# Linear attention into a bilinear FFN on one core: k loads ahead of q, later scores of two units, a half out product ahead of a deferred one

## The chip, the core and the metric

The kernel runs on one core of one Trainium2 chip. The engines are TensorE (PE, matmuls; PEld is its weight load), VectorE (DVE), ScalarE (ACT), GpSimd (POOL) and SyncE (SP, which here issues nearly all DMAs). The metric is device microseconds of one execution; several executions are timed and the median is given. One execution was profiled, and all durations below are from it. Its span is the time from its first to its last instruction.

## The reference

There are 4 batches, 8 heads, 768 positions and a head size of 64. Attention is linear with a decay `lam` of each head and a running state over blocks of positions; the result, 3072 rows of 512, goes through a bilinear FFN of width 1536.

```python
for b in range(nb):                       # blocks of 64 positions
    intra = einsum('bhic,bhjc->bhij', qb, kb) * Dmask        # lam ** (i - j), lower triangle
    intra = einsum('bhij,bhjd->bhid', intra, vb)
    inter = einsum('bhid,bhde->bhie', qb * lam_pow, kv_state)
    out[:, :, sl] = intra + inter
    kv_state = lam_block * kv_state + einsum('bhsd,bhse->bhde', kb * rev_pow, vb)
x = out.transpose(0, 2, 1, 3).reshape(3072, 512)
return (x @ w_a) * (x @ w_b) @ w_out
```

## The kernel before

**Units and groups.** The 3072 rows are cut into 24 units of 128 rows (six to a batch). `GROUPS = (4, 1, 2, 4, 4, 4, 4, 1)` joins them for the FFN: group 0 has units 0 to 3, group 1 unit 4, group 2 units 5 and 6, groups 3 to 6 four units each (7 to 10, 11 to 14, 15 to 18, 19 to 22), group 7 unit 23. While the FFN of one group runs on PE, the attention of later units is woven in, so that the xT of a group (its attention result, transposed, as the matmuls take it) is ready when its FFN begins.

**The attention of a unit.** `P` in the plan is `prep_k` and `prep_v`. `prep_k` scales k and then q with powers of lam (L401, on POOL from unit 6 on) into one bf16 tile `qk`. For units 7 to 23 (`DMA_T`) it then issues a transposing DMA on SP (L429) that gives `qkT`. `prep_v` casts v (L420) and calls `pump`, which issues further loads on SP from the list `pending`, as far ahead as `LOOKAHEAD` lets it. Units 4 to 6 are transposed by PE (`T`, L443) and copied by ACT (L445). `S` is the scores: eight matmuls (L457) into two PSUM banks, then two masking multiplies on DVE (L480; with `MASK_ACT` one bank goes through a copy by ACT, L471, first). `V` updates the state (L527) and copies it. `O2` takes two units: matmuls with the state and with the masked scores (L497), then two casts into xT on ACT (L520). `Q` does this for units 7 and 8 together with the scores of 9 and 10.

**The FFN of a plain group (0, 1, 2, 7).** For each of twelve column blocks f: four matmuls with w_a into one PSUM bank, a cast by ACT (L605), four matmuls with w_b, a multiply on DVE into `ab` (L623). `ps_bank` hands out seven PSUM banks in rotation, and a matmul waits until the bank's former reader is done. Then come the out products (L643), twelve matmuls of 128x512 for each unit.

**The FFN of groups 3 to 6** (`ffn_z`) works on four units as a 2x2 block product with seven products instead of eight. It takes sums of weights (`WS`, `weight_sum`, L269 to L275, eight of them), sums of xT (`X`, `x_sums`, L713 to L726), and, for groups 4 to 6, sums of out weights (`WO`) and of the product (`SM`, `ab_sum`, L843 to L849). For each of six columns n, PE runs product 1 into U, 4 into V, 0 into W, 5 into U, 6 into V, 3 into U (L748, four matmuls of 128x256 each); ACT copies U and V in between into tiles of a pool of seven (`snap`, L829), and DVE subtracts such a copy from the finished bank (L777, L787, L789). Product 2 into U, the last of a column, is deferred into the next column: `last_product` is kept in `fin`, runs after the next column's product 5 (after its product 1 in "joined" groups), and ends with ACT's cast (L754) and DVE's multiply (L756). The out products of groups 4 to 6 are also seven products, each in two halves (`H`, `out_half`, L870, six matmuls of 128x256), woven into the next group; a group in which they are woven is joined.

**What sets the order.** Each engine runs its instructions in the order of the program, and that order is written out by hand: `PLAN` says at which slot of a group's FFN which piece of attention, sum or store is issued. In a plain group the slots 0 to 11 follow the column blocks and the later ones the parts of the out products; in groups 3 to 6 a column has three slots, the last three follow from 18 on. `WS_ENG` and its like say which engine takes a sum.

**Kept rows.** The FFN results of units 0 to 4 are copied by ACT into tiles of the same pool `snap` (`o_kept`, L634) and are stored only when the plan says `W` (`store_kept`, L629, on SP). Until such a store has landed, its tile can't be used for another copy of U or V.

Of the kernel before, what the change touches and what calls it, by code (L numbers as in the profile page):

```python
# [22 lines left out]
def _bc(ap, dims):  # L23
# [9 lines left out]
DMA_T = range(7, 24)  # L33
# [73 lines left out]
XS_ENG = {(3, 0): 'dve', (3, 1): 'dve', (3, 2): 'dve', (4, 0): 'dve', (4, 1): 'dve', (4, 2): 'dve', (5, 0): 'dve', (5, 1): 'pool', (5, 2): 'pool', (6, 0): 'pool', (6, 1): 'pool', (6, 2): 'pool'}  # L107
WS_ENG = {0: 'dve', 1: 'dve', 2: 'dve', 3: 'dve', 4: 'dve', 5: 'dve', 6: 'dve', 7: 'pool'}
WO_ENG = {0: 'dve', 1: 'dve', 2: 'pool', 3: 'dve', 4: 'dve'}
# [4 lines left out]
def kernel(  # L114
# [183 lines left out]
    for u in range(n0 + 1, NU):  # L298
        pending += [("q", u), ("k", u), ("v", u)]
    used = {"u": 0}  # L300
# [340 lines left out]
    def out_mms(op, ab, t, fs, lo=0, hi=d_model):  # L641
        for f in fs:
            nc.tensor.matmul(op[:, lo:hi], lhsT=ab[:, f, t * 128:(t + 1) * 128],  # L643
                             rhs=wo_sb[:, f, lo:hi], start=(f == 0), stop=(f == FC - 1))

    def ffn(u0, n, xT, hook, first, last):
# [36 lines left out]
        for t in range(n):  # L683
            op = ps_bank("op", [128, d_model], F32, ffn=True)
            if last and t == n - 1:
                for lo, hi in ((0, 256), (256, 384), (384, 512)):
                    if lo:
                        op = ps_bank("op", [128, d_model], F32, ffn=True)
                    out_mms(op, ab, t, range(FC), lo, hi)
                    store(u0 + t, op, lo, hi, nc.scalar if hi == d_model else None)  # L690
                return
            out_mms(op, ab, t, range(FC // 2))
            hook(FC + 2 * t)
            out_mms(op, ab, t, range(FC // 2, FC))
            store(u0 + t, op, 0, d_model)
            hook(FC + 2 * t + 1)
# [35 lines left out]
    def ffn_z(g, u0, xT, hook, joined, own):  # L732
# [27 lines left out]
        for n in range(NP):  # L760
# [5 lines left out]
            if joined:  # L766
                if fin:
                    fin.pop()()
                hook(3 * n)
# [332 lines left out]
```

## Time and profile before

| what | value |
|---|---|
| median of 3 timed runs | 224.38 us (224.23 to 226.21) |
| the profiled execution's own time | 223.83 us |
| its span | 222.1 us |
| PE busy | 213.9 us (96%) |
| DVE, ACT, POOL busy | 165.3, 122.7, 99.8 us |
| granted clock of TensorE | 1.000 |
| HBM read, written | 28.32 MB, 6.29 MB |
| DMA engines' busy share, 60 to 120 us | 1.20 to 1.26 |
| loads of q, k, v: each, issue to landing | 256 KB, 4.6, 4.7, 4.9 us |

A share of the DMA engines over 1 means that packets overlap on an engine. In a timeline a line gives the start and the length of a group of like instructions in us, engine, source line, operation, the tile written and the tiles read, how many, and in brackets the idle time of the engine just before, when it is over 0.15 us, with what ended it. Ends of matmuls are modelled, so starts are compared with starts. A few matmul records can be missing, so that a group may show one less than it has.

### The profile page before, as it was taken

Reading aid. Unit: us, or ns where it says so; the run is one execution under the profiler, and the core shown is the slowest. Engines: PE = TensorE matmul, PEld = TensorE weight load, DVE = VectorE, ACT = ScalarE, POOL = GpSimd, SP = SyncE. Lnnn points to the kernel's source line nnn. Section 1 sums busy time; section 2 is a strip of 40 time slices with the busy share of each in tenths; the row PEclk is TensorE's granted clock in tenths of the full one; section 3 lists DMA queues with packets and bytes.
Section 4 is the critical chain, followed back from the end, with each engine's and each line's share of the span. In section 5 each row is a group of like instructions: output and inputs, shape, how many; then the busy total and the mean of one; then the engine's idle time right before and its main releaser. Section 6 shows DMA issues by size and latency. Waiting matters only on the chain.

```text
span 222.1 us, 5601 instructions
## 1 busy us (share of the span) xinstructions
PE 213.9 (96%) x2225; PEld 159.0 (72%) x2235; DVE 165.3 (74%) x272; ACT 122.7 (55%) x249; POOL 99.8 (45%) x95
## 2 busy tenths in 40 slices
PE   7899999999999999999999999899999999999994
PEld 2476444448678657787547888688888888888994
DVE  0994773968798668889888889968688865777540
ACT  3686446038454266775356988776535666543322
POOL 6061004246795175540559559786417722051100
PEclk9999999999999999999999999999999999999999
DMA  4999999999999999999999999652021100112042
GB/s 132 321 265 349 356 387 344 277 216 218 216 204 220 232 174 248 190 275 245 180 248 236 233 201 211 138 101 50 0 88 56 52 0 4 47 47 97 0 145 94
DMA packets 99081, 39.42 MB, mean 177 GB/s; under 512 B 85488, under 2 KB 95088, under 8 KB 99056
## 3 DMA queue, kind: packets, MB, share of 16 engines
q1 hardware_dynamic: 98768, 39.00, 79.8%
q8 instruction: 17, 0.28, 0.6%
q10 hardware_dynamic: 288, 0.07, 0.1%
q14 instruction: 8, 0.07, 0.1%
HBM read 28.32 MB, written 6.29 MB: 156 GB/s over the span
## 4 chain that ended last, share of the span: by engine, by line
PE 67%; DMA 16%; SPq 5%; DVE 5%; ACT 2%; issue 2%; POOL 1%; ACTq 0%; DVEq 0%; POOLq 0%
PE U L748 17%; PE op L870 12%; PE V L748 9%; DMA wst<-in_moe_w_b_dram 8%; PE b_ps L596 5%; PE op L810 5%; PE a_ps L596 5%; PE W L748 4%; PE op L643 3%; DMA kf<-in_k_dram 3%; DMA k<-in_k_dram 3%; PE o_ps L497 3%; PE kq L457 2%; DMA out_dram<-o_kept 2%; SPq L187 1%
## 5 line engine op out<-in xcount | busy, mean ns | idle before, releaser
L829 ACT COPY u<-U 128x512 f32<-128x512 f32 x48 | 28.3, 590 | 16.5 <-PE U L748 16.4
L401 POOL TENSOR_TENSOR qk<-kf,lp_k 128x512 bf16<-128x512 f32 x18 | 19.5, 1084 | 33.7 <-DMA kf<-in_k_dram 18.9
L623 DVE TENSOR_TENSOR ab<-a_sb,b_ps 128x128 bf16<-128x128 bf16 (+2 forms) x48 | 19.2, 417 | 13.6 <-ACT a_sb L605 10.2
L596 PE MATMUL a_ps<-xT,wa_sb 128*128 128x128 bf16 (+2 forms) x198 | 27.6, 267 | 0.5 <-DVE wa_sb L244 0.2
L480 DVE TENSOR_TENSOR m<-kq,lotri 128x512 bf16<-128x512 f32 x40 | 25.6, 682 | 3.1 <-PE kq L457 3.0
L596 PE MATMUL b_ps<-xT,wb_sb 128*128 128x128 bf16 (+2 forms) x192 | 27.5, 272 | 0.2
L756 DVE TENSOR_TENSOR ab<-oab 128x1024 bf16<-128x1024 bf16 x24 | 19.0, 791 | 11.3 <-ACT oab L754 11.1
L401 POOL TENSOR_TENSOR qk<-qf,lp_q 128x512 bf16<-128x512 f32 x20 | 24.8, 1242 | 1.7 <-DMA qf<-in_q_dram 1.7
L605 ACT CAST a_sb<-a_ps 128x128 bf16<-128x128 f32 (+2 forms) x48 | 17.3, 374 | 14.7 <-PE a_ps L596 14.4
L643 PE MATMUL op<-wo_sb,ab 128*128 128x512 bf16 (+2 forms) x114 | 21.8, 334 | 0.5 <-issue 0.3
L596 PEld LDWEIGHTS <-wa_sb 128*128 128x128 bf16 x200 | 16.7, 98 | 6.6 <-issue 0.5
L748 PEld LDWEIGHTS <-wz_a 128*128 128x128 bf16 x192 | 18.2, 98 | 3.9 <-issue 0.9
L748 PEld LDWEIGHTS <-wz_b 128*128 128x128 bf16 x192 | 18.7, 98 | 2.2
L596 PEld LDWEIGHTS <-wb_sb 128*128 128x128 bf16 x192 | 15.8, 98 | 6.2 <-issue 0.2
L748 PE MATMUL U<-xT,wz_a 128*128 128x256 bf16 x96 | 18.3, 272 | 0.0
L748 PE MATMUL U<-xT,wz_b 128*128 128x256 bf16 x96 | 18.3, 272 | 0.0
L520 ACT CAST xT<-o_ps 128x512 bf16<-128x512 f32 (+1 forms) x24 | 12.2, 554 | 10.7 <-PE o_ps L497 10.5
L787 DVE TENSOR_TENSOR oab<-U,u 128x512 bf16<-128x512 f32 x24 | 16.3, 681 | 0.8 <-PE U L748 0.8
L420 POOL CAST vb<-vf 128x512 bf16<-128x512 f32 x14 | 10.2, 730 | 13.8 <-DMA vf<-in_v_dram 13.8
L748 PEld LDWEIGHTS <-wa_sb 128*128 128x128 bf16 x144 | 13.4, 98 | 4.0 <-issue 1.0
L643 PEld LDWEIGHTS <-ab 128*128 128x128 bf16 x120 | 10.1, 98 | 8.5
L754 ACT CAST oab<-U 128x512 bf16<-128x512 f32 x24 | 14.2, 592 | 3.5 <-PE U L748 3.5
(130 smaller groups left out, 453.1 us busy)
## 6 DMA issues: line engine op xcount, KB each, us to landing
vf<-in_v_dram SPq DMA_DIRECT2D x24, 256.0 KB, 4.9
qf<-in_q_dram SPq DMA_DIRECT2D x20, 256.0 KB, 4.6
kf<-in_k_dram SPq DMA_DIRECT2D x20, 256.0 KB, 4.7
out_dram<-o_sb SPq DMA_DIRECT2D x18, 256.0 KB, 2.4
wst<-in_moe_w_a_dram SPq DMA_DIRECT2D x6, 512.0 KB, 8.8
wst<-in_moe_w_b_dram SPq DMA_DIRECT2D x6, 512.0 KB, 9.2
wst<-in_moe_w_out_dram SPq DMA_DIRECT2D x6, 512.0 KB, 10.7
out_dram<-o_kept SPq DMA_DIRECT2D x5, 256.0 KB, 4.3
```

Source lines behind the costliest of these rows:

```text
L401: eng_of(eng).tensor_mul(dst.rearrange("p (c b) d -> p b c d", b=2), x[:].rearrange("p (b c) d -> p b c d", b=2), lp.rearrange("p (b c) o ...
L480: nc.vector.tensor_mul(m, kq[i], lotri_bc)
L596: nc.tensor.matmul(ps[:, lo:hi], lhsT=w_sb[:, s, f * 128:(f + 1) * 128], rhs=xT[:, s, lo:hi], start=(s == 0), stop=(s == KS - 1), skip_gro ...
L605: nc.scalar.copy(a_sb[:, :gt], ps[:, :gt])
L623: nc.vector.tensor_mul(ab[:, f, :gt], a_sb[:, :gt], ps[:, :gt])
L643: nc.tensor.matmul(op[:, lo:hi], lhsT=ab[:, f, t * 128:(t + 1) * 128], rhs=wo_sb[:, f, lo:hi], start=(f == 0), stop=(f == FC - 1))
L748: nc.tensor.matmul(ps[:, k, :], lhsT=wt[:, s, n * 128:(n + 1) * 128], rhs=rhs[i][:, s, :], start=(fresh and k == 0 and s == 0), stop=True, ...
L754: nc.scalar.copy(oab[:, 0], U)
L756: nc.vector.tensor_mul(ab[:].rearrange("p (h i) (t c) -> p h i t c", h=2, t=2)[:, :, n], o5[:, :, :, 0, :], o5[:, :, :, 1, :])
L787: nc.vector.tensor_sub(oab[:, 1], U, v1)
L829: nc.scalar.copy(t, ps)
L870: nc.tensor.matmul(ps[:, t, :], lhsT=lhs[p][:, n, t * 128:(t + 1) * 128], rhs=rhs[:, n, :], start=fresh, stop=True, skip_group_check=True)
```

## The change

- **Weight sums.** Sum 5 moves from slot 0 of group 1 to the end of that group's last slot, sums 6 and 7 move from there into group 2 (slots 9 and 13), and sum 7 runs on DVE instead of POOL.
- **Group 1's out products** run as 4 + 4 + 4 matmuls instead of 6 + 6. The last slot of the group (scalings of unit 8, O2 of 5 and 6, state of 6, sum 5) comes ahead of the last four. The transposes of unit 6 come ahead of the scores of unit 5.
- **Kept stores.** The third follows the first two in slot 2 of group 2; the fourth and fifth move from the end of group 2 to slot 21 of group 3.
- **Group 3.** Scores 11, scores 12 and O2 of 11 and 12 each move one slot on.
- **Groups 4 and 5.** The scalings of unit 22 come ahead of the sums (4, 0) and (4, 2); sum (4, 0) moves from slot 16 to 17, sum (4, 4) from the last slot of group 4 into slot 0 of group 5. The first half out product (4, 0) gets a new slot -1: in group 5's first column it comes ahead of the deferred last product of group 4.
- **Loads.** For units 7 to 23, k is loaded ahead of q.

```diff
 PLAN = {
-    1: [(0, 'PV', 5), (0, 'WS', 5), (3, 'T', 5), (4, 'PK', 6), (6, 'PV', 6), (9, 'P', 7),
-        (11, 'S', 5), (11, 'T', 6), (12, 'S', 6), (13, 'P', 8), (13, 'O2', (5, 6)), (13, 'V', 6),
-        (13, 'WS', 6), (13, 'WS', 7)],
-    2: [(2, 'W', None), (2, 'W', None), (3, 'P', 9), (4, 'V', 7), (4, 'S', 7),
-        (6, 'V', 8), (10, 'PK', 10), (11, 'PV', 10), (11, 'P', 11), (11, 'W', None),
+    1: [(0, 'PV', 5), (3, 'T', 5), (4, 'PK', 6), (6, 'PV', 6), (9, 'P', 7),
+        (11, 'T', 6), (11, 'S', 5), (12, 'S', 6), (13, 'P', 8), (13, 'O2', (5, 6)), (13, 'V', 6), (13, 'WS', 5)],
+    2: [(2, 'W', None), (2, 'W', None), (2, 'W', None), (3, 'P', 9), (4, 'V', 7), (4, 'S', 7),
+        (6, 'V', 8), (9, 'WS', 6), (10, 'PK', 10), (11, 'PV', 10), (11, 'P', 11),
         (11, 'S', 8), (11, 'P', 12), (12, 'Q', (7, 8, 9, 10)), (13, 'P', 13),
-        (13, 'W', None), (13, 'V', 9), (14, 'XA', 3), (14, 'O2', (9, 10)), (14, 'X', 3), (15, 'W', None)],
-    3: [(1, 'S', 11), (5, 'S', 12), (8, 'O2', (11, 12)), (10, 'P', 14), (12, 'S', 13),
+        (13, 'V', 9), (13, 'WS', 7), (14, 'XA', 3), (14, 'O2', (9, 10)), (14, 'X', 3)],
+    3: [(2, 'S', 11), (6, 'S', 12), (9, 'O2', (11, 12)), (10, 'P', 14), (12, 'S', 13),
         (15, 'P', 15), (17, 'WO', 0), (17, 'S', 14), (18, 'V', 13), (18, 'WO', 1),
-        (19, 'P', 16), (19, 'O2', (13, 14)), (20, 'P', 17), (21, 'S', 15), (21, 'P', 18),
+        (19, 'P', 16), (19, 'O2', (13, 14)), (20, 'P', 17), (21, 'S', 15), (21, 'P', 18), (21, 'W', None), (21, 'W', None),
         (24, 'WO', 2), (25, 'WO', 3), (25, 'WO', 4), (25, 'X', 4)],
     4: [(0, 'S', 16), (1, 'V', 15), (3, 'S', 17), (4, 'O2', (15, 16)), (4, 'P', 19),
         (6, 'P', 20), (6, 'S', 18), (10, 'O2', (17, 18)), (10, 'X', 5), (11, 'S', 19),
-        (13, 'P', 21), (16, 'SM', (4, 0)), (17, 'SM', (4, 2)), (17, 'P', 22), (17, 'S', 20),
-        (17, 'SM', (4, 4))],
-    5: [(0, 'SM', (4, 1)), (1, 'H', (4, 0)), (1, 'V', 19), (2, 'O2', (19, 20)),
+        (13, 'P', 21), (16, 'P', 22), (17, 'SM', (4, 0)), (17, 'SM', (4, 2)), (17, 'S', 20)],
+    5: [(-1, 'H', (4, 0)), (0, 'SM', (4, 1)), (0, 'SM', (4, 4)), (1, 'V', 19), (2, 'O2', (19, 20)),
...
-WS_ENG = {0: 'dve', ..., 6: 'dve', 7: 'pool'}
+WS_ENG = {0: 'dve', ..., 6: 'dve', 7: 'dve'}
...
     for u in range(n0 + 1, NU):
-        pending += [("q", u), ("k", u), ("v", u)]
+        pending += [("k", u), ("q", u), ("v", u)] if u in DMA_T else [("q", u), ("k", u), ("v", u)]
...
+            if n == 1:
+                out_mms(op, ab, t, range(4))
+                hook(FC)
+                out_mms(op, ab, t, range(4, 8))
+                hook(FC + 1)
+                out_mms(op, ab, t, range(8, FC))
+                store(u0 + t, op, 0, d_model)
+                return
             out_mms(op, ab, t, range(FC // 2))
             hook(FC + 2 * t)
...
             if joined:
-                if fin:
-                    fin.pop()()
+                if n == 0:
+                    hook(-1)
+                fin.pop()()
                 hook(3 * n)
```

More of the change, by code (lines that the diff above doesn't have):

```diff
@@ L107 @@
 XS_ENG = {(3, 0): 'dve', (3, 1): 'dve', (3, 2): 'dve', (4, 0): 'dve', (4, 1): 'dve', (4, 2): 'dve', (5, 0): 'dve', (5, 1): 'pool', (5, 2): 'pool', (6, 0): 'pool', (6, 1): 'pool', (6, 2): 'pool'}
-WS_ENG = {0: 'dve', 1: 'dve', 2: 'dve', 3: 'dve', 4: 'dve', 5: 'dve', 6: 'dve', 7: 'pool'}
+WS_ENG = {0: 'dve', 1: 'dve', 2: 'dve', 3: 'dve', 4: 'dve', 5: 'dve', 6: 'dve', 7: 'dve'}
 WO_ENG = {0: 'dve', 1: 'dve', 2: 'pool', 3: 'dve', 4: 'dve'}
```

## The prediction

> **What bounds the kernel now.** I read the page's busy line and chain first.
>
> ```profile
> PE 213.9 (96%) x2225; PEld 159.0 (72%) x2235; DVE 165.3 (74%) x272; ACT 122.7 (55%) x249; POOL 99.8 (45%) x95
> PE 67%; DMA 16%; SPq 5%; DVE 5%; ACT 2%; issue 2%; POOL 1%; ACTq 0%; DVEq 0%; POOLq 0%
> ```
>
> TensorE (PE) is busy for 213.9 of 222.1 us, and the edits add and remove no matmul. So the change can win only where PE waits, and can lose only by new waits. Next I went through PE's timeline from 50 to 145 us, the stretch the edits lie in, and compared each group's start with the start of the same group where nothing waits. Four places stand out; the rest is dense.
>
> ```profile
> 53.63 0.39 PE L596 MATMUL a_ps<-xT,wa_sb 128*128 128x128 bf16 x4
> 54.13 0.38 PE L596 MATMUL b_ps<-xT,wb_sb 128*128 128x128 bf16 x4
> ...
> 62.28 0.40 PE L527 MATMUL kvd<-vb,qk 128*128 128x128 bf16 x4
> 62.80 0.87 PE L596 MATMUL a_ps<-xT,wa_sb 128*128 128x256 bf16 x4
> 63.51 0.60 PE L596 MATMUL b_ps<-xT,wb_sb 128*128 128x256 bf16 x4
> ...
> 88.03 0.38 PE L748 MATMUL U<-z_sub,wb_sb 128*128 128x256 bf16 x2
> 88.75 0.38 PE L748 MATMUL V<-z_add,wz_a 128*128 128x256 bf16 x2 [0.34 <-ACT u L829]
> ...
> 140.01 0.38 PE L748 MATMUL U<-xT,wz_b 128*128 128x256 bf16 x2
> 141.20 0.38 PE L748 MATMUL U<-z_sub,wa_sb 128*128 128x256 bf16 x2 [0.81 <-DVE oab L787]
> ```
>
> A group of four 128x128 matmuls normally starts 0.22 us after the one before it (51.18, 51.40, 51.62), a pair of 128x256 too, four 128x256 take 0.44 (63.95 to 64.38). So PE loses 0.28 at 54.13, 0.30 + 0.27 at 62.80 and 63.51, 0.50 at 88.75, 0.97 at 141.20: 2.32 in all. The timelines of the other engines tell why.
>
> ```profile
> 52.48 1.39 DVE L273 TENSOR_TENSOR wz_b<-wb_sb,wz_b 128x1536 bf16<-128x1536 bf16 x1
> 61.39 2.70 DVE L420 CAST vb<-vf 128x512 bf16<-128x512 f32 x1
> 82.07 0.43 DVE L718 TENSOR_TENSOR z_sub<-xT 128x512 bf16<-128x512 bf16 x1 [1.59 <-ACT xT L520]
> 140.00 0.55 DVE L843 TENSOR_TENSOR zab<-ab 128x768 bf16<-128x768 bf16 x1
> 140.47 0.68 DVE L787 TENSOR_TENSOR oab<-U,u 128x512 bf16<-128x512 f32 x1
> ```
>
> ```profile
> 61.58 0.58 ACT L634 COPY o_kept<-op 128x512 f32<-128x512 f32 x1 [2.01 <-PE op L643]
> 62.17 1.07 ACT L520 CAST xT<-o_ps 128x512 bf16<-128x512 f32 x2
> 84.95 0.58 ACT L829 COPY u<-U 128x512 f32<-128x512 f32 x1 [0.20 <-PE U L748]
> 88.11 0.58 ACT L829 COPY u<-V 128x512 f32<-128x512 f32 x1 [0.83 <-DMA out_dram<-o_kept]
> ```
>
> ```profile
> 60.71 3.09 POOL L275 TENSOR_TENSOR wz_b<-wb_sb 128x1536 bf16<-128x1536 bf16 x1
> ```
>
> ```profile
> 79.26 2.08 SPq L429 DMA_TRANSPOSE qkT<-qk  x1
> 83.72 1.03 SPq L629 DMA_DIRECT2D out_dram<-o_kept  x1
> ```
>
> The reader is to see: a weight sum stands ahead of the ab multiplies at 52.48; the kept row's copy stands ahead of both xT casts at 61.58; the third kept store leaves SP only at 83.72, and the fifth snapshot of group 3 waits for its buffer; the half sum zab stands ahead of the oab subtraction that the deferred last product needs.
>
> **The change, part by part.** "Local" times are those of before.
>
> A. Weight sum 5 (b, third sum) leaves slot 0 of group 1. The b_ps group at 54.13 takes the bank of column block 1, whose multiply stood behind the 1.39 us sum (it ran at 53.80). Without it the next constraint is the bank of the transposes of unit 5, copied by ACT from 53.84 for 1.01, needed at 54.97 in the new time: just free. -0.28; bounds -0.28 and 0. The sum now stands behind group 1's masks at about 62.5, where DVE no longer has the 2.70 us cast: that cast ended at 64.09, 0.29 after POOL's sum at 60.71 (to 63.80), which goes to DVE.
>
> B. Group 1's out products run 4+4+4 instead of 6+6, with units 5 and 6 and their xT casts ahead of the last four and of the kept copy. The casts (1.07) start when PE's o_ps are done and lie beside kvd (0.32) and four 128x512 (24 take 5.19 at 111.80, so 0.86 for four). Transposes of unit 6 ahead of scores 5 change no count of shape changes. -0.57, of which 0.05 may stay as the kept copy (0.58) must free its bank before the second a_ps: -0.55; bounds -0.57 and -0.2.
>
> C. The third kept store follows the first two at about 68.5, on SP ahead of two transposes, and lands long before 88: -0.50, nothing left over. Its SP time (0.5, as its neighbours) delays transposes 9 and 10; they landed at 73.0 and 74.0, their scores stand at 76.26, so it is hidden, with over 1 us to spare.
>
> D. Scores 11 move from slot 1 to slot 2 of group 3. In each column PE runs product 5 into U, product 6 into V, product 3 into U, and the last waits until ACT has copied U after product 5 (84.95 to 85.53). Scores 11 took 0.33 (84.85 to 85.18) in between. Without them PE comes to product 3 at 85.20, waits to about 85.6, and pays the 0.33 afterwards: +0.33; bounds 0 and +0.42. Scores 12 and the pair 11/12 move within later columns, where the deferred last product of the column before (0.44) lies in that place: 0.
>
> E. Start of group 5. Sum (4,0) goes behind the two subtractions (0.47 off DVE's way), and out half (4,0), 0.65 on PE, is put ahead of the deferred product. PE then does the half from 140.22 to 140.88, and the subtraction, started at 140.00 instead of 140.47, is done at 140.65: the 0.97 wait is gone. But the half used to cover the copy of V: the deferred product now ends at 141.32, ACT's cast of it starts 0.25 later as before (141.88 after 141.63), the copy of V runs from 142.05 to 142.64, and product 6 into V would be due at 142.42: 0.26 wait, and 0.05 more at product 3. -0.66; bounds -0.97 and -0.3. Unit 22's scalings ahead of sum (4,2) on POOL fill its 1.54 wait before 140.63, and sum (4,4) waits for (4,2), which ends near 143.4, behind the masks: 0.
>
> F. Weight sums 6 and 7 on DVE in group 2. The first falls into gaps of 0.45 between multiplies, with seven PSUM banks in rotation: 0. The second (0.95) falls into the 1.59 idle before 82.07, so alone it is free. But sums from SBUF wait for a running POOL instruction: z_mix at 82.56 took 1.12 and ended 0.29 after POOL's q scaling (82.09 to 83.39). Unit 12's scalings (1.04 + 1.30) come about then. Bounds 0 and +0.9 (sum, z_add and z_sub each one POOL instruction late, less 0.93 until the V product at 83.43); I take +0.3, since most of the 1.59 is free.
> The Trainium skill ("SBUF — State Buffer", Who interferes with whom) states that a VectorE instruction with two SBUF inputs and a GpSimd instruction that reads SBUF exclude each other, the later one blocked in full. The trace agrees (2.70 for the cast under the 3.09 sum). By that rule alone the sum on DVE would also hold up unit 12's scalings, and F would be at its +0.9.
>
> G. k ahead of q for units 7 on. Same bytes; POOL waited 18.9 us for k in all, and with k first it scales k while q lands. At 77.19 both scalings waited for k (landed 77.03, q 75.82); swapped, the second ends near 78.2 instead of 79.23, about 1.0 sooner, less 0.64 for the third store, now ahead (the first two landed 0.64 apart). PE's scores wait for transposes: unit 11's landed 5.0 after 79.26, at 84.2, and scores 11 are now due at 85.3 (84.85, plus two products of 0.44 and D's wait of 0.4, less A and B). The last two kept stores go from 95.28 and 96.89 to behind unit 18's transpose, ahead of unit 19's, which landed at 131.1 with its scores at 132.87. Same bytes ahead of it in both. 0; bounds 0 and +1.1.
>
> Sum: -0.28 - 0.55 - 0.50 + 0.33 - 0.66 + 0.30 = -1.36. The span of 222.10 becomes 220.74; with the 1.73 around it (223.83 - 222.10) the profiled time would be 222.47. The median shown, 224.38, lies 0.55 above the profiled execution, so on that scale I say 223.0.
>
> **The rivals.**
> 1. All waits go and nothing new comes: D hidden, E in full, F nothing: -0.28 - 0.57 - 0.50 - 0.97 = -2.32, 222.1. For it: the edits meet just the four waits. Against it: both new waits follow from ACT rows that took 0.58 to 0.60 everywhere.
> 2. The gain is taken by transposes. The DMA share is over 1 from 40 to 140 us; if the last stores (1.10 of SP at 95.28) delay unit 19's transpose by 2.2, it lands at 133.3 and scores 19, due near 132.2 (132.87 less A to D and F), wait 1.1: 224.38 - 1.36 + 1.1 = 224.1. Against it: the same bytes have left the queue earlier.
> 3. Slower: DVE comes late to group 3's sums. Weight sum 7 waits for a k scaling (1.04), z_add for a q scaling (1.30), z_sub for a vb cast (0.80), z_mix for the next k scaling (1.04); with its own 0.95 that is 5.1, less 1.59 idle and 0.93 slack: 2.6 of PE wait. It decides from 1.66 (the sum without F). 224.38 - 1.66 + 2.6 = 225.3. For it: z_mix and the 2.70 cast above. Against it: POOL itself waited 1.3 to 2.4 between units there.
>
> **How the numbers follow.** Forecast 0.56; rival 1 0.20; rival 2 0.13; rival 3 0.11. The range 221.9 to 224.9 takes in rivals 1 and 2 and the bounds, and leaves most of rival 3 out. A measurement of this kernel tells about 1% from no change (2.24 us: 222.14 and 226.62). Faster by over 1%: most of rival 1 and the forecast's lower edge, 0.22. Slower by over 1%: rival 3 at more than its price, 0.06. Within: 0.72.
>
> **What would show it.** PE's timeline: no late b_ps in group 1 (A), a_ps of group 2 right behind four op matmuls (B), no wait on an o_kept DMA (C), about 0.4 ahead of product 3 in group 3's first column (D), in group 5's first column no wait at the deferred product and 0.2 to 0.3 at product 6 (E). F is wrong if V's first product of group 3 waits for z_sub over 0.9 or not at all. G is wrong if PE waits at scores 11 or 19. A wait after 150 us that before did not have would overturn the whole.

## The result and the profile after

The changed kernel takes 225.84 us in the median of 20 executions (224.49 to 229.47), the kernel before 224.16 (20 executions, 223.5 to 226.21). The ratio is 1.0068, with a 95% interval of 1.0045 to 1.0091: slower by 0.7%, where 0.6% faster was forecast, and above the range. The ratio leaves out executions more than 1.5% above the fastest of the same kernel (seven of e7's twelve are left, and too few of e17's for a ratio); since those turn out to be the kernel's own doing, medians of all executions stand beside ratios below. Seven of the 20 show a mean granted clock of 0.993 or less and 227.6 us or more; the other 13 have a median of 225.07.

The profiled execution is the shortest (224.49 us, span 222.8, against 223.83 and 222.1). First its busy line and chain, from its page:

```profile
PE 214.2 (96%) x2225; PEld 159.0 (71%) x2235; DVE 167.4 (75%) x273; ACT 122.2 (55%) x249; POOL 97.4 (44%) x94
PE 86%; DMA 5%; SPq 3%; DVE 2%; ACT 2%; issue 1%; ACTq 0%; DVEq 0%
```

Then PE's timeline. Here L594, L754, L877 and L836 are the L596, L748, L870 and L829 of before, L399 and L418 its L401 and L420; L455, L762, L760 and L794 are its L457, L756, L754 and L787.

```profile
54.24 0.39 PE L594 MATMUL b_ps<-xT,wb_sb 128*128 128x128 bf16 x4
...
62.63 0.60 PE L594 MATMUL a_ps<-xT,wa_sb 128*128 128x256 bf16 x4
63.07 0.60 PE L594 MATMUL b_ps<-xT,wb_sb 128*128 128x256 bf16 x4
...
85.22 0.38 PE L754 MATMUL U<-xT,wz_a 128*128 128x256 bf16 x2 [0.18 <-ACT u L836]
...
85.80 0.40 PE L455 MATMUL kq<-qkT 64*128 64x128 bf16 x8
...
88.32 0.38 PE L754 MATMUL V<-z_add,wz_a 128*128 128x256 bf16 x2
...
140.88 0.38 PE L754 MATMUL U<-z_sub,wa_sb 128*128 128x256 bf16 x2 [0.25 <-DVE oab L794]
...
142.55 0.39 PE L754 MATMUL U<-z_mix,wz_a 128*128 128x256 bf16 x2 [0.64 <-ACT u L836]
...
143.52 0.38 PE L754 MATMUL V<-z_add,wz_a 128*128 128x256 bf16 x2
```

The waits that the prediction set out from are gone or smaller: b_ps follows the a_ps at 54.01 by 0.23, b_ps at 63.07 follows in 0.44, V at 88.32 doesn't wait, and the bracket at the deferred product is 0.25 instead of 0.81. By starts of the same matmuls, the changed kernel was 0.38 us late at 50.68 (it began late, ahead of all edits), 0.45 early at 63.50, still 0.45 early at 94.72, and 0.13 late at 143.52; from there on it stays at 0.13 to 0.19 late, and 0.5 more comes between the last matmul and the end. So the first edits won 0.83, group 3 gave back what the kept store won, and group 5's start lost 0.58. The other timelines say why there (the line of before first, then DVE, POOL and ACT of the changed kernel):

```profile
139.39 0.69 DVE L756 TENSOR_TENSOR ab<-oab 128x1024 bf16<-128x1024 bf16 x1 [0.41 <-ACT oab L754]
```

```profile
138.97 1.25 DVE L762 TENSOR_TENSOR ab<-oab 128x1024 bf16<-128x1024 bf16 x1 [0.40 <-ACT oab L760]
140.14 0.68 DVE L794 TENSOR_TENSOR oab<-U,u 128x512 bf16<-128x512 f32 x1
```

```profile
138.63 1.04 POOL L399 TENSOR_TENSOR qk<-kf,lp_k 128x512 bf16<-128x512 f32 x1
```

```profile
141.39 0.62 ACT L416 CAST vb<-vf 128x512 bf16<-128x512 f32 x1 [2.46 <-DMA vf<-in_v_dram]
141.91 0.58 ACT L836 COPY u<-U 128x512 f32<-128x512 f32 x1
```

Unit 22's scalings, moved ahead, now run beside the multiply at 138.97, which takes 1.25 instead of the 0.69 it took at 139.39 before; and the cast of unit 22's v holds ACT for 2.46 us until v has landed (141.37; before, 139.25), with group 5's first copy of U behind it, so that PE loses 0.80 ahead of product 5 (142.55). This accounts for the profiled execution. It does not account for those of 227 to 229 us.

### The profile page after: what moved, and what is told of

Same layout as the page of the kernel before. It is cut to its first block, busy times and chain, and to the rows that moved or that the text cites. A ratio compares the mean times of both kernels' runs of the same rounds, so it can differ in the third digit from the quotient of the medians.

```text
span 222.8 us, 5613 instructions
## 1 busy us (share of the span) xinstructions
PE 214.2 (96%) x2225; PEld 159.0 (71%) x2235; DVE 167.4 (75%) x273; ACT 122.2 (55%) x249; POOL 97.4 (44%) x94
## 4 chain that ended last, share of the span: by engine, by line
PE 86%; DMA 5%; SPq 3%; DVE 2%; ACT 2%; issue 1%; ACTq 0%; DVEq 0%
PE U L754 18%; PE op L877 12%; PE a_ps L594 9%; PE b_ps L594 9%; PE V L754 9%; PE op L641 9%; PE W L754 5%; PE op L817 5%; PE o_ps L495 4%; PE kq L455 3%; DMA wst<-in_moe_w_a_dram 3%; SPq L185 2%; DMA q<-in_q_dram 2%; PE kvd L525 1%; ACT u L836 1%
## 5 line engine op out<-in xcount | busy, mean ns | idle before, releaser
L836 ACT COPY u<-U 128x512 f32<-128x512 f32 x48 | 28.3, 590 | 17.1 <-PE U L754 16.0
L399 POOL TENSOR_TENSOR qk<-kf,lp_k 128x512 bf16<-128x512 f32 x18 | 21.2, 1177 | 32.7 <-DMA kf<-in_k_dram 22.1
L594 PE MATMUL a_ps<-xT,wa_sb 128*128 128x128 bf16 (+2 forms) x198 | 27.4, 267 | 0.6 <-DVE wa_sb L242 0.5
L762 DVE TENSOR_TENSOR ab<-oab 128x1024 bf16<-128x1024 bf16 x24 | 20.0, 834 | 10.2 <-ACT oab L760 10.1
L594 PE MATMUL b_ps<-xT,wb_sb 128*128 128x128 bf16 (+2 forms) x192 | 27.5, 272 | 0.1
L399 POOL TENSOR_TENSOR qk<-qf,lp_q 128x512 bf16<-128x512 f32 x20 | 22.8, 1141 | 2.3 <-DMA qf<-in_q_dram 1.7
L754 PEld LDWEIGHTS <-wz_a 128*128 128x128 bf16 x192 | 18.2, 98 | 4.9 <-ACT u L836 0.9
L594 PEld LDWEIGHTS <-wa_sb 128*128 128x128 bf16 x200 | 16.7, 98 | 6.6 <-DVE wa_sb L242 0.7
L754 PEld LDWEIGHTS <-wz_b 128*128 128x128 bf16 x192 | 18.7, 97 | 2.2
L594 PEld LDWEIGHTS <-wb_sb 128*128 128x128 bf16 x192 | 15.7, 98 | 6.0
L754 PE MATMUL U<-xT,wz_a 128*128 128x256 bf16 x96 | 18.3, 272 | 0.2 <-ACT u L836 0.2
L754 PE MATMUL U<-xT,wz_b 128*128 128x256 bf16 x96 | 18.3, 272 | 0.0
L418 POOL CAST vb<-vf 128x512 bf16<-128x512 f32 x14 | 10.6, 754 | 15.2 <-DMA vf<-in_v_dram 14.8
L794 DVE TENSOR_TENSOR oab<-U,u 128x512 bf16<-128x512 f32 x24 | 16.4, 681 | 0.7 <-PE U L754 0.7
L754 PEld LDWEIGHTS <-wa_sb 128*128 128x128 bf16 x144 | 13.3, 97 | 3.5 <-issue 0.4
L760 ACT CAST oab<-U 128x512 bf16<-128x512 f32 x24 | 14.2, 592 | 2.6 <-PE U L754 2.6
```

The costliest lines, as they stand in the source:

```text
L399: eng_of(eng).tensor_mul(dst.rearrange("p (c b) d -> p b c d", b=2), x[:].rearrange("p (b c) d -> p b c d", b=2), lp.rearrange("p (b c) o ...
L594: nc.tensor.matmul(ps[:, lo:hi], lhsT=w_sb[:, s, f * 128:(f + 1) * 128], rhs=xT[:, s, lo:hi], start=(s == 0), stop=(s == KS - 1), skip_gro ...
L754: nc.tensor.matmul(ps[:, k, :], lhsT=wt[:, s, n * 128:(n + 1) * 128], rhs=rhs[i][:, s, :], start=(fresh and k == 0 and s == 0), stop=True, ...
L760: nc.scalar.copy(oab[:, 0], U)
L762: nc.vector.tensor_mul(ab[:].rearrange("p (h i) (t c) -> p h i t c", h=2, t=2)[:, :, n], o5[:, :, :, 0, :], o5[:, :, :, 1, :])
L794: nc.vector.tensor_sub(oab[:, 1], U, v1)
```

## The experiments

Each group ran beside the kernel before on one chip; "low" counts executions with a mean clock of 0.993 or less, "over" those above 226 us at a higher clock; both are called long. The second column is the median of before in the same group. Of its 138 executions in these groups, 4 are low and 9 over.

| run | before | median (lowest to highest), executions | low | over | ratio, 95% |
|---|---|---|---|---|---|
| changed kernel | 224.16 | 225.84 (224.49 to 229.47), 20 | 7 | 3 | 1.0068 [1.0045, 1.0091] |
| e1 | 224.99 | 226.94 (224.66 to 230.75), 12 | 4 | 4 | 1.0041 [1.0006, 1.0077] |
| e2 | 224.99 | 225.16 (223.93 to 227.0), 12 | 0 | 4 | 1.0030 [0.9998, 1.0061] |
| e3 | 224.99 | 225.17 (223.8 to 229.57), 12 | 2 | 2 | 1.0014 [0.9984, 1.0044] |
| e4 | 224.99 | 225.21 (222.97 to 227.99), 12 | 1 | 2 | 1.0000 [0.9970, 1.0029] |
| e5 | 224.91 | 224.46 (223.11 to 229.19), 12 | 1 | 1 | 0.9973 [0.9941, 1.0005] |
| e6 | 224.91 | 225.62 (224.64 to 229.4), 12 | 5 | 0 | 1.0026 [0.9984, 1.0069] |
| e7 | 224.91 | 225.65 (222.49 to 227.71), 12 | 1 | 5 | 0.9973 [0.9927, 1.0019] |
| e8 | 224.91 | 230.5 (229.3 to 232.24), 6 | 6 | 0 | 1.0236 [1.0183, 1.0289] |
| e9 | 225.05 | 227.07 (224.87 to 229.49), 12 | 3 | 5 | 1.0075 [1.0036, 1.0114] |
| e10 | 225.05 | 223.82 (223.35 to 229.5), 12 | 1 | 0 | 0.9949 [0.9921, 0.9977] |
| e11 | 225.05 | 224.15 (223.4 to 225.46), 12 | 0 | 0 | 0.9974 [0.9943, 1.0005] |
| e12 | 225.05 | 228.92 (223.41 to 232.1), 12 | 8 | 2 | 0.9986 [0.9930, 1.0043] |
| e13 | 224.84 | 225.6 (223.94 to 227.1), 12 | 0 | 6 | 1.0049 [1.0020, 1.0079] |
| e14 | 224.84 | 225.24 (222.68 to 226.74), 12 | 1 | 3 | 0.9967 [0.9933, 1.0000] |
| e15 | 224.84 | 227.74 (225.8 to 228.7), 6 | 4 | 1 | 1.0114 [1.0072, 1.0155] |
| e16 | 224.84 | 224.89 (224.12 to 232.75), 12 | 1 | 1 | 1.0002 [0.9979, 1.0025] |
| e17 | 224.53 | 228.69 (224.99 to 229.58), 6 | 4 | 0 | none |

### e1 to e4: the cast, the stores, the half product

**e1.** The changed kernel with `(16,'P',22)` in group 4 made `(16,'PK',22)`, and `(2,'PV',22)` added in group 5.

> The changed kernel with one step split: unit 22's value cast (ACT) leaves slot 16 of group 4 and stands in group 5's slot 2, behind the first column's four copies of U and V; its q and k scalings and every DMA stay as they are. Theory 'cast': the cast of unit 22 waits on ACT for its load (landed 141.37 in the profiled run) and holds the first copy of U of group 5 by about 0.5 us, so PE loses 0.64 + 0.25 + 0.30 there, and in other executions, where the load lands later still, 1 to 3 us. It expects the waits at the deferred product's successor (product 6 into U) to fall to about 0.25, a median of 223.2 to 224.0 where the changed kernel has 225.8 and the kernel before 224.2, and the spread of the executions (224.5 to 229.5 in the changed kernel) to come down to about 1.5 us. Theory 'cover' (half (4,0) ahead of the deferred product uncovers copies by itself): no change beyond 0.3 us, 225.5 to 226. Theory 'clock' (the later executions are long because of a lower granted clock that has nothing to do with the cast): some executions still at clock 0.985 to 0.992 and 227 to 229 us, in the same share.

It didn't help: 226.94. The profiled execution (226.2 us) has 0.27 ahead of V in group 5's first column but now loses 1.26 by starts ahead of scores 19, whose transpose landed at 134.15 (132.09 in the changed kernel, 131.07 before):

```profile
134.19 0.40 PE L455 MATMUL kq<-qkT 64*128 64x128 bf16 x8 [1.19 <-DMA qkT<-qk]
```

The cast is one place at which a late queue shows, not the cause.

**e2.** The changed kernel with the last two `W` back in group 2, slots 13 and 15.

> The changed kernel with its last two kept stores put back where they stood before, group 2's slots 13 and 15; the third stays with the first two. Theory 'stores': the two stores, issued at 123.4 and 124.4 ahead of unit 19's transpose, move the whole queue from there on by about 1 us (transpose 19 landed 132.09 where before had 131.07, v of unit 22 141.37 where before had 139.25), and that is why the cast of unit 22 comes late on ACT. It expects v of unit 22 to land at 139.3 to 140.3, no wait at group 5's first copy beyond 0.3, and a median near 224.0. Theory 'order of k and q' (k ahead of q makes v late, not the stores): v of unit 22 still at 141 or later, 225.5 or more. Theory 'cover': v early, but the waits of PE at group 5's first column stay, 225.5 or so.

Median 225.16 beside 224.99, no execution at a low clock. Transpose 19 landed at 131.79, 1.4 ahead of its scores, v of unit 22 at 140.08, and ACT waits 0.45 for it instead of 2.46. In the medians most of the loss is gone with it, in the ratio (1.0030) about half, and four executions over 226 at full clock remain that the late stores can't explain.

**e3.** The kernel before with only the kept stores moved (third to slot 2 of group 2, the others to slot 21 of group 3).

> The kernel before with the moves of the kept stores alone: the third with the first two at slot 2 of group 2, the fourth and fifth behind unit 18's transpose in group 3. Theory 'stores': the snapshot's wait of group 3 (0.50) goes, but the late stores push the loads by 1 us; unit 22's cast stands late enough in this order (slot 17 behind the snapshot) that PE feels it only in part: 223.7 to 224.8, with more spread than before if the late queue is what makes the long executions. Theory 'cast' alone: 223.7 (0.5 won, nothing lost). If the executions here spread to 227 to 229 as those of the changed kernel do, the deferred stores are the cause of the spread and the cast's place in ACT's order is not.

No gain (225.17), though the wait at the snapshot of group 3 is gone: transpose 19 landed at 132.21, v of unit 22 at 141.25, and PE loses 0.43 at group 5's first product 5 instead. In this profile the gain of an early third store is eaten by the late two.

**e4.** The kernel before with only the edits of groups 4 and 5.

> The kernel before with the edits at the end of group 4 and the start of group 5 alone: unit 22's scalings and cast at slot 16, the sums (4,0) and (4,4) behind the subtractions, and half (4,0) ahead of the deferred product. Loads and stores as before, so v of unit 22 is to land near 139.3. Theory 'cast': with v there in time nothing holds ACT, the wait of 0.97 goes and 0.3 to 0.6 of copies is uncovered: 223.5 to 223.9. Theory 'cover': no gain or a loss of its own, 224.2 to 225.5, with PE waits at the products 6 of group 5's first column although v of unit 22 landed early.

No change: ratio 1.0000. The profile shows the wait of 0.97 turned into 0.66 at the deferred product and 0.27 ahead of V: 0.04 won.

### e5 to e8: the queue

**e5.** The changed kernel with the last two stores out of the busy stretch altogether:

```
-  3: ... (21,'P',18), (21,'W',None), (21,'W',None), ...
+  3: ... (21,'P',18), ...
+  5: ... (5,'W',None), (5,'W',None), (5,'S',21), ...
```

> The changed kernel with its last two kept stores taken out of group 3 and issued in slot 5 of group 5, some 20 us later, where the queue is nearly empty; nothing else moves. Theory 'queue': from 40 to 140 us the transfers are a second chain nearly as long as PE's; transpose 19 and v of unit 22 landed 1.8 us ahead of their use in the kernel before and 0.3 us or less in the changed one, because 1 us of store went in just ahead of them and PE came 0.5 sooner, so every stall of the queue now goes through to PE. It expects transpose 19 to land at 130.8 to 131.3 and v of unit 22 at 138.5 to 139.5, no wait of PE at scores 19, and a median 1 us or more below that of the changed kernel (223.3 to 224.5), with few executions over 226. Theory 'half' (the half product ahead of the deferred one and unit 22's cast on ACT lose the time, whatever the queue does): 225 to 226. Theory 'order of loads' (k ahead of q): 225 to 226 too.

Nearly as the theory of the queue had it: transpose 19 at 131.49, v of unit 22 at 139.70, each 0.2 later than expected, no wait at scores 19, 224.46 beside 224.91. One execution is still at a low clock (229.19 us, 0.992).

**e6.** The changed kernel with the edits of groups 4 and 5 undone.

> The changed kernel with the edits at the end of group 4 and the start of group 5 undone: unit 22's scalings and cast at slot 17 behind the sum (4,0), half (4,0) back in slot 1, no hook ahead of the deferred product. The late stores stay. Theory 'queue': unit 19's transpose still lands at 132 or later and the long executions stay, 225 to 226. Theory 'half': the loss goes with these edits, and with the waits won in groups 1 to 3 the median is 223.2 to 224.0 with the spread of the kernel before.

Those edits are not the cause: 225.62, five of twelve at a low clock. The profile loses 0.98 at the deferred product as before, and 1.13 at group 5's first product 5: ACT waited 2.68 us for v of unit 22 (landed 141.47) there too, with the cast back in its old place.

**e7.** The changed kernel with `pending += [("q", u), ("k", u), ("v", u)]` for all units.

> The changed kernel with the loads of units 7 on in the old order, q ahead of k. Theory 'order of loads' (with k first the transposes of units 8 to 12 land 1 to 2 us later, as they did: 71.8 for 69.3, 75.1 for 73.0, 85.75 for 84.2): these land at the times of before, scores 11 and 12 wait no more, and the median falls by 0.5 to 1 us, 224.8 to 225.3. Theory 'queue' with the late stores as the cause: the early transposes may come sooner, but by 132 us the queue is as late as with k first, and the median stays at 225.3 to 226.

The median hardly moves (225.65), but the kind of long execution does: five over 226 at full clock, and the one at 0.992 took only 223.72 us. The early transposes stay late (units 8 and 11 landed at 72.42 and 86.03), so the order of loads is not the only thing that delays them.

**e8.** The kernel before with a second `dma_start` of the same tile in `store_kept` when fewer than two rows are left.

> The kernel before, with its last two kept rows stored twice in place, that is two more stores of 0.26 MB at 95 to 98 us in the queue and nothing else changed on any engine. Theory 'queue': the queue has 1.8 us to spare ahead of transpose 19; two more stores take about 1.3 us, so the profiled execution alone may show little, but more executions go over 226 us, as in the changed kernel: median 224.8 to 226. If the queue has room there (it waited for scalings at 104 to 107), the same as before: 224.2 to 225.0, and the place of the stores, not their number, would be what counts.

230.5, but not for the reason expected: each second store left SP only after the first had landed (95.70, 100.37, 101.25, 104.14), so it held the queue and did not only lengthen it. Unit 14's transpose landed at 107.75 instead of 102.05. As a test of the bytes it is void; it shows what a long wait of PE brings. First PE's timeline, then the stretch behind the wait (length, busy time of PE, PEld, DVE, ACT and POOL, granted clock, DMA share, GB/s):

```profile
107.80 0.40 PE L457 MATMUL kq<-qkT 64*128 64x128 bf16 x8 [3.08 <-DMA qkT<-qk]
```

```profile
107.80:112.20 4.40, 4.35 (x21) 2.00 (x22) 1.93 (x3) 0.58 (x1) 1.36 (x2) 0.61 1.25 236
```

After 3.1 us without work PE has 4.4 us at a mean clock of 0.61, which costs 1.7 more. All six executions of e8 have a clock of 0.991 to 0.993. So the low clock of the long executions suggests that PE stood still for long somewhere in them.

### e9 to e12: on one chip, and a long execution seen

**e9.** The changed kernel once more.

> The changed kernel itself once more, beside variants of it on the same chip. Expected as before: 225 to 226.5 median, some 4 in 10 executions over 226.2, and in the profile transpose 19 landing at 132 or later and v of unit 22 at 141 or later. If it comes out at 224.5 here, the loss was that chip's and not the kernel's.

227.07 beside 225.05: the loss is the kernel's. This time the profile shows a long execution (227.79 us, clock 0.992), and transpose 19 is not late in it (130.78, ahead of a PE that has lost more). DVE's timeline, then POOL's, then PE's, then two stretches as in e8:

```profile
113.40 1.80 DVE L288 TENSOR_TENSOR wy<-wo_sb 128x1536 bf16<-128x1536 bf16 x1
115.12 1.52 DVE L730 TENSOR_TENSOR z_sub<-xT 128x1024 bf16<-128x1024 bf16 x1
116.57 1.09 DVE L731 TENSOR_TENSOR z_add<-xT 128x1024 bf16<-128x1024 bf16 x1
117.59 3.30 DVE L732 TENSOR_TENSOR z_mix<-xT 128x512 bf16<-128x512 bf16 x1
```

```profile
113.27 1.11 POOL L399 TENSOR_TENSOR qk<-kf,lp_k 128x512 bf16<-128x512 f32 x1 [1.74 <-DMA kf<-in_k_dram]
114.35 1.75 POOL L399 TENSOR_TENSOR qk<-qf,lp_q 128x512 bf16<-128x512 f32 x1
116.05 1.07 POOL L418 CAST vb<-vf 128x512 bf16<-128x512 f32 x1
117.08 3.52 POOL L288 TENSOR_TENSOR wy<-wo_sb 128x1536 bf16<-128x1536 bf16 x1
```

```profile
120.94 0.39 PE L754 MATMUL U<-z_mix,wz_a 128*128 128x256 bf16 x2 [2.61 <-DVE z_mix L732]
```

```profile
117.60:120.90 3.30, 0.73 (x12) 0.32 (x6) 3.30 (x3) 0.63 (x2) 3.30 (x2) 1.00 1.37 250
120.90:124.40 3.50, 3.46 (x20) 2.68 (x21) 2.23 (x4) 1.22 (x3) 1.89 (x2) 0.55 1.16 176
```

Each x sum of group 4 on DVE ends 0.3 to 0.5 after the POOL instruction beside it: z_sub with unit 18's q scaling, z_add with its v cast, z_mix with the out-weight sum wy, 3.30 us for a sum of 0.43. PE loses 2.77 by starts and then 3.5 x 0.45 = 1.6 to the clock. The Trainium skill ("SBUF — State Buffer", Who interferes with whom) states that a VectorE instruction with two SBUF inputs contends with a GpSimd instruction that reads SBUF, and the trace agrees (3.30 beside 3.52). In the kernel before and in the short execution of the changed one they meet differently; z_sub and unit 18's k scaling stand like this, before first (DVE, POOL), then changed (DVE, POOL):

```profile
114.84 0.68 DVE L724 TENSOR_TENSOR z_sub<-xT 128x1024 bf16<-128x1024 bf16 x1
```

```profile
115.25 1.17 POOL L401 TENSOR_TENSOR qk<-kf,lp_k 128x512 bf16<-128x512 f32 x1 [2.50 <-DMA kf<-in_k_dram]
```

```profile
114.42 1.53 DVE L730 TENSOR_TENSOR z_sub<-xT 128x1024 bf16<-128x1024 bf16 x1
```

```profile
113.81 1.59 POOL L399 TENSOR_TENSOR qk<-kf,lp_k 128x512 bf16<-128x512 f32 x1 [2.13 <-DMA kf<-in_k_dram]
```

Before, z_sub starts 0.41 ahead of the k scaling, z_add shares its time with that scaling and z_mix with the q scaling: two POOL instructions, the v cast and then wy, are still to come. In the changed kernel k lands 1.5 sooner (113.59 for 115.09), POOL starts it 1.44 sooner while DVE's sums come only 0.42 sooner, z_sub meets the k scaling and z_mix the v cast. One instruction further, as in e9, and z_mix meets wy. What takes it one further is DVE's own sum of out weights: in e9 the second of them (113.40) starts 0.13 behind the k scaling (113.27) and takes 1.80 instead of 0.95, so that each sum behind it meets the next POOL instruction. In the changed kernel's short execution that sum starts 0.26 ahead of the k scaling, in the kernel before 1.28 ahead.

**e10.** e5 with the loads back in the order q, k, v.

> The changed kernel with its last two kept stores in slot 5 of group 5 (as in the fifth experiment) and, besides, the loads back in the order q, k, v. Theory 'stores alone': the order of q and k counts for nothing, 224.3 to 224.7 as with the moved stores alone. Theory 'order too': k first costs the early transposes 1 to 2 us and with it scores 11 and product 3 of group 3, so 0.3 to 0.5 less: 223.8 to 224.3.

The best version: 223.82 beside 225.05, ratio 0.9949. In its profile z_sub is again ahead of the k scaling (114.97 against 115.24).

**e11.** The kernel before with the kept stores alone moved as in e5.

> The kernel before with its third kept store up with the first two and its fourth and fifth in slot 5 of group 5; nothing else. Theory 'queue': the snapshot's wait of 0.50 goes and the queue gains 1 us or more of room by 131 us, where the third experiment (same early third store, but the last two put ahead of transpose 19) gained nothing. Expected 223.8 to 224.5, and hardly any execution over 226. If the place of the two stores doesn't count, the same as in the third experiment, 225.2 beside 225.0.

224.15 beside 225.05, none of twelve over 225.46, where e3 with its late stores won nothing and had four of twelve over 226. This speaks for the place of the two stores, though the ratios' intervals overlap (0.9943 to 1.0005, and 0.9984 to 1.0044).

**e12.** e5 with scores 11 and 12 and their pair back in slots 1, 5 and 8 of group 3.

> The changed kernel with its last two kept stores in slot 5 of group 5 and scores 11 and 12 and their pair back in slots 1, 5 and 8 of group 3. The prediction had scores 11 cover the copy of U (0.33); the trace of the changed kernel shows 0.35 of wait there, but also scores 11 waiting 0.15 for their transpose in their later place. If the cover counts, the wait of 0.35 ahead of product 3 goes; if the transpose of unit 11 (landed 85.8) is what is late, scores 11 in the earlier place wait 0.5 to 1 us for it, and nothing is won: 224.3 to 224.9.

Scores 11 wait 1.30 for their transpose (landed 86.52) at 86.57, so the cover that the old place gave is not to be had here. That k first is the reason isn't shown: with q first (e10) the same transpose landed at 85.54, in the changed kernel at 85.75. More than expected: eight of twelve are at a low clock (228.92 us in the median of all), and the profiled one has the same meeting, z_mix 3.30 at 119.34 beside wy 3.52 at 118.83.

### e13 to e17: the meeting, and what brings it about

**e13.** The changed kernel with `(24,'WO',2)` moved to `(8,'WO',2)` of group 4 and `WO_ENG[2]` from pool to dve.

> The changed kernel with its third out-weight sum (wy, 3.3 us on GpSimd at 117.8, beside the x sums of group 4) made on DVE in slot 8 of group 4, where DVE has 0.6 us idle. Theory 'meeting' (the long executions, 227 to 229.5 at clock 0.992, are those in which z_mix of group 4 stands behind wy): none of the 12 executions has a clock below 0.996 from this place, the highest are 226 to 227 (transpose 19 late in some of them, which this does not mend), median 224.7 to 225.5 where the changed kernel has 226 to 227. Theory 'queue alone': the long executions stay in their share, 4 or more of 12.

No execution at a low clock, none above 227.1. Six are over 226 at full clock. The late queue, which this leaves as it was, would account for them, but e13's own profile (223.94 us) is not one of them.

**e14.** e10 with the same move of wy.

> The changed kernel with the last two kept stores in slot 5 of group 5, loads in the order q, k, v, and the wy sum on DVE in slot 8 of group 4. Theory 'meeting' with 'queue': both causes of long executions are gone, 223.3 to 224.0 median, none over 225.5 (the tenth experiment, without the last part, had one of 12 at 229.5 and the rest at 223.35 to 224.55). If the DVE sum costs something of its own in slot 8, up to 0.5 more than the tenth.

Not better than e10. The profiled execution (226.74) shows a new meeting: wy on DVE pushed z_sub of group 5 to 134.03, where it took 2.61 beside POOL's z_add, and the deferred product waited 1.0 for the subtraction behind it.

**e15** and **e16.** One pair swapped on POOL, in the changed kernel and in the kernel before; no other engine's order differs:

```
-  (21,'P',18), ... (24,'WO',2),
+  (21,'PK',18), (21,'WO',2), (21,'PV',18), ...
```

> The changed kernel with one pair of instructions on GpSimd swapped: the wy sum ahead of the cast of v of unit 18 instead of right behind it; all other engines and SP as they are. In the changed kernel's profile DVE's three x sums of group 4 each wait for one GpSimd instruction, z_sub for the k scaling, z_add for the q scaling, z_mix for the v cast; with wy in the cast's place z_mix meets it nearly every time. Theory 'meeting': PE waits about 2.8 us ahead of U from z_mix in almost every execution and then has about 3.6 us at half clock: median 227.5 to 229, clock 0.992. Theory 'queue alone': the cast is 3.3 us later and the sum sooner, nothing else: no change, or less than 0.5.

> The kernel before with the same pair swapped: wy ahead of the cast of v of unit 18. In its profile z_sub of group 4 runs before unit 18's k scaling starts (114.84 against 115.25), z_add waits for that scaling and z_mix for the q scaling; so GpSimd is one instruction further back against DVE, and wy would still come after z_mix. Theory 'meeting', with k ahead of q (k lands 1.2 us sooner and GpSimd starts on it at 113.8 instead of 115.25) as the edit that brought the two together: little change, 224.5 to 225.5, with at most 3 of 12 executions at clock 0.992. If it also goes to 228, the place of GpSimd against DVE was no better in the kernel before, and the edit to the order of loads isn't what made the meeting likely.

They come out in opposite ways: 227.74 with four of six at a low clock in the changed kernel, 224.89 with one of twelve (232.75) in the one before. The "nearly every time" was too much; e15's own profile (227.32 us at full clock) is an execution in which z_mix came ahead of wy, and PE lost 1.44 to a late copy by ACT instead. Nor do six executions tell four low ones from the changed kernel's ten of 32 (with e9).

**e17.** The kernel before with k ahead of q for units 7 on, and nothing else of the change.

> The kernel before with the loads of units 7 on in the order k, q, v and nothing else changed. Theory 'order of loads': k of unit 18 lands about 1.2 us sooner, GpSimd starts unit 18's scalings earlier against DVE's x sums of group 4 (in the kernel before z_sub came 0.41 ahead of the k scaling; here the k scaling is expected to start ahead of z_sub by up to 1 us), and some executions slip one instruction further, to z_mix behind wy: 2 to 5 of 12 at clock 0.993 or less and 227 us or more, median 224.8 to 226. Theory 'other edits' (only the waits won in groups 1 to 3 or the early third store bring the two together): as the kernel before, 224.5 to 225.2, at most 1 of 12 long.

228.69 beside 224.53; four of six at clock 0.992 or 0.993 and 228.6 to 229.6 us, none of eleven in the kernel before. In the profile, a short execution (225.6), POOL is one instruction ahead, as expected:

```profile
116.02 1.35 POOL L401 TENSOR_TENSOR qk<-kf,lp_k 128x512 bf16<-128x512 f32 x1 [2.55 <-DMA kf<-in_k_dram]
```

```profile
116.39 1.53 DVE L724 TENSOR_TENSOR z_sub<-xT 128x1024 bf16<-128x1024 bf16 x1
```

Over all runs with wy in its place, kernels with k first have 32 of 98 executions at a low clock (the changed kernel, e1, e2, e5, e6, e9, e12, e17); with q first it is 5 of 60 (e3, e4, e7, e10, e11) and 4 of 138 in the kernel before. That the order of loads alone makes long executions is shown by e17; that the meeting is what makes them long, by the profiles of e9 and e12 and by e13, which has none. No long execution of e17 itself was profiled.

In e9 and e12 the k scaling starts 0.13 and 0.17 ahead of DVE's second sum of out weights; in the other profiles with k first (changed kernel, e1, e2, e5, e6, e17) it starts 0.15 to 0.58 behind it, with q first (before, e3, e4, e7, e10, e11) 0.53 to 1.70. So the meeting is decided by some tenths of a microsecond, and the start alone varies by as much. Why the share among the kernels with k first runs from none of twelve (e2) to eight (e12) is open: e17, with four of six, has 0.50 in its profile, e2 0.58. With q first too, in e3 and e11, POOL's k scaling comes ahead of z_sub, and two and none of twelve are low, so that place alone doesn't make an execution long.

## Why the prediction was wrong

**A and B right.** 0.27 and 0.56 were won (forecast 0.28 and 0.55).

**C right, D right.** The wait of 0.50 is gone. Product 3 of group 3's first column waits 0.35 (by starts, 84.65 to 85.22), as D said. Scores 11 lose 0.05 more behind it (85.80 is 0.36 after 85.44, where 0.31 is usual); their transpose landed at 85.75, 1.5 later than before, where G's sum of 1.0 less 0.64 had it 0.4 sooner. Which edit made it late is open.

**E right in kind, too large by more than half.** Unit 22's scalings were priced at 0 because they fill an idle stretch of POOL. Beside the moved scaling DVE's multiply grew by 0.56, so the subtraction started at 140.14 and not at 140.00, and PE still loses 0.43 by starts at the deferred product. Where v of unit 22 is in time (e5, e10) the step wins about 0.25 instead of 0.66; alone in the kernel before (e4) 0.04. That the changed kernel's profile loses 0.58 there all the same is not E's doing: 0.80 is lost ahead of product 5, behind the load of v, and e6, with the cast in its old place, has ACT waiting 2.68 us for the same load. That loss belongs to G.

**F: not seen.** V's first product of group 3 doesn't wait for z_sub at all (83.06, 0.22 behind the group ahead of it), which by the prediction's own sign makes F wrong, though the weight sum took 1.30 and the later z_add and z_sub 1.27 and 1.26 beside POOL's scalings. The 0.3 was not spent. (The cast of 2.70 that F sets beside its rule has one input, not two; z_mix with its 1.12 is the row with two.)

**G is the step that failed.** Both its parts were priced at 0 (bounds 0 and +1.1).
- *k ahead of q* was followed to the transposes alone. It also moves POOL's scalings of unit 18 by 1.0 us against DVE's x sums (from 0.41 behind z_sub's start to 0.61 ahead of it; by 0.8 in e17), and the rule that F itself cites makes each of these sums wait for the POOL instruction beside it. Rival 3 had this mechanism but put it in group 3 and laid it to weight sum 7; the place is group 4, the trigger the loads, and the price in a long execution 2.8 us and then about 1.6 of clock.
- *The late kept stores*, "same bytes ahead of it in both": the bytes are the same, the room is not. Without the two stores the queue is only 0.4 sooner at 101 to 124 us (transposes 14 and 18 landed 0.45 and 0.39 sooner), since SP also waits for scalings (4.2 us between 95 and 142); with them back at 123, transpose 19 lands 1.0 later than before and v of unit 22 2.1. That was nearly all the room there was: transpose 19 landed 1.8 us ahead of its scores before, 0.36 in the changed kernel, 1.4 in e2 and e5, whose two stores stand elsewhere. This is rival 2, right in kind; e1's profile shows its wait of 1.26, and the profiles of e2, e5 and e11 don't have it.

The rest of the sum was nearly right: as measured, A to F come to -0.27 - 0.56 - 0.50 + 0.35 + 0.05 - 0.25 = -1.18, where -1.36 was forecast, and with q first and the two stores out of the way (e10) the kernel gains 1.23 in the medians.

The forecast counted what PE gains. A PE that comes 0.8 us sooner also comes that much closer to the queue and to POOL, and the sum has no term for it.

## What to carry to other kernels

When a load, a cast or a scaling is moved, list every instruction on the engine that takes it, and look at what runs beside each of them on the engine that can hold it up (here POOL for DVE), not only at who waits for the result. In a kernel whose engines run in order, look for the longest instruction in such a place (here wy, 3.1 to 3.5 us) and ask how many instructions away the other engine is; one that is a single instruction away is a lottery that one profile of a short execution will not show, so compare all executions and their clocks. Stores that nobody waits for belong where the queue is empty: with two of them ahead of unit 19's transpose the early third store won nothing (e3), with the same two 20 us later 0.9 us in the medians (e11, its interval just reaching no change), and with that and the old order of loads the changed kernel becomes 0.5% faster than the one before (e10).

## What was not expected of the hardware

- A wait of PE of 2.77 us (e9) or 3.15 (e8), by starts, was followed by 3.5 to 4.4 us at a mean granted clock of 0.55 to 0.61; waits of 1.26 (e1) and 1.44 (e15) were not. The Trainium skill ("TensorE: Matmul & The Clock Gate", Why this matters for your kernels) says that gaps over about 3 us bring PE to half clock; the traces agree in kind, and here 2.77 was enough.
- The exclusion of DVE and POOL goes on from one instruction to the next: four sums in a row on DVE each ended with a POOL instruction (e9), so that being one instruction late costs the length of whatever stands next on POOL.
